# Attention decode: moving P V of one group among the score sums of the next, with K loads one tile ahead at the end

## The chip, the cores and the metric

One core of one Trainium2 chip. Times are device microseconds (us) of one execution. Fast runs are compared with fast runs; the record gives every run of this study as fast. A ratio is the mean time of one kernel's fast runs over that of the kernel before in the same rounds, with a 95% interval, so it is not quite the ratio of the medians quoted beside it. Times inside a profile are counted from the start of its span, the profiled execution. The chain of a page is the work that ended last, followed back step by step to what each piece waited for.

## The reference, cut to what matters

```python
q = (x @ wq).reshape(B, Sq, H, Dh)...          # B=8, Sq=1, H=32, Dh=128
scores = einsum("bhqd,bhkd->bhqk", q, k_cache) * Dh ** -0.5      # k_cache: 8 x 32 x 4096 x 128, bf16
p = softmax(scores)
o = einsum("bhqk,bhkd->bhqd", p, v_cache)                        # v_cache: the same size
a = o.reshape(B, Sq, H * Dh) @ wo
b = gelu(layernorm(x) @ w1 + b1) @ w2 + b2
return g * a + (1 - g) * b                     # g = sigmoid(sum(x * gate_w))
```

K and V are 537 MB together; the four weight matrices (wq, wo, w1, w2) add 20 MB. All of it is read once.

## The kernel before

It works in 64 groups, each of one batch row and 4 heads. A group has a K tile and a V tile of 4 MB (128 partitions, 128 tokens of 128 values each). There are two K buffers and two V buffers. All large loads are issued by SyncE in program order, and each waits until its buffer is free:

```python
def load_k(g):                       # waits for the last product of group g-2
    k_land[g] = op("sync", ... KB[g % 2] <- K, [k_done.get(g - 2)] ...)
def load_v(g):                       # waits for the last P V matmul of group g-2
    t = op("sync", ... VB[g % 2] <- V, [v_done.get(g - 2)] ...)
```

The scores of a group go in four batches. VectorE multiplies K by q (`mult`, 2.28 us), TensorE adds the products up with eight identity matmuls, and VectorE finishes the sum (`reduce`). Then come the softmax, P V and its reduction to one row a head:

```python
def scores(g, between=lambda: None):
    mult(g, 0)
    mult(g, 1)
    for c in range(NCK):             # NCK = 4
        reduce(g, c)
        if c == 0:
            between()                # normalises group g-1
        if c + 2 < NCK:
            mult(g, c + 2)
...
def pv(g):
    ... 32 matmuls P^T V, the first waits for V, the exponentials and the PSUM bank (accumulators) ...
    v_done[g] = p_pv[g]
    ... total (ones x row sums), eviction to O_sb on ScalarE, gather (8 small matmuls) ...
...
for g in range(NG):                  # NG = 64; cut
    ... load_k(g); load_v(g)   (g == 62: load_k(62), load_k(63), load_v(62), V63 in pieces)
    scores(g, between)
    q_of(g + 1)
    softmax(g)                       # 4 exponentials on ScalarE
    ... up projection in groups 2 to 13, down projection in groups 18 to 23 ...
    pv(g)
```

TensorE's order is thus sums of g, P V of g, sums of g+1.

## Time and profile before

| | before |
|---|---|
| median of the first 3 runs (range) | 1367.1 us (1364.4 to 1367.9) |
| span of the profiled run | 1359.6 us |
| busy: TensorE, VectorE, ScalarE | 69%, 61%, 16% |
| mean DMA rate | 410 GB/s |
| last V lands / end | 1340.1 / 1359.6 us |

The prediction below shows the lines of the profile that matter: the chain of waits, the costliest groups, one turn of the loop, and the windows at the end. One line on SyncE, from the waits of the DMA queue of the kernel before (who waited, for whom, total us, times, longest), is of use later:

```profile
SPq L213 <- PE psb L381: 547.6, 59, 10.0
```

SyncE stands in front of a V load (L213) until P V has given the buffer back. The wait alone is no loss, since earlier loads are still running meanwhile. What matters is how far ahead of their end the next load is issued.

### The profile page before, as it was taken

The numbers are of one execution on the slowest core, as the hardware profiler recorded it, in microseconds if no ns is written. First come the engines' busy times: TensorE is split into PE (matmuls) and PEld (weight loads), VectorE is DVE, ScalarE is ACT, GpSimd is POOL, SyncE is SP. The second block draws the span as 40 slices with busy tenths as digits, with TensorE's granted clock in tenths as the row PEclk, the third lists the DMA queues.
The fourth block names the chain that finished last, engine by engine and source line by source line (L and its number), as shares of the span: only waits on it lengthen the run. The fifth ranks groups of instructions, "written<-read, shape, count | busy, mean of one in ns | idle before, by whom it ended". The sixth has DMA issues, their size and how long they took to land.

```text
span 1359.6 us, 12287 instructions
## 1 busy us (share of the span) xinstructions
PE 931.5 (69%) x5166; PEld 420.5 (31%) x5166; DVE 823.9 (61%) x992; ACT 212.0 (16%) x650; POOL 1.8 (0%) x10
## 2 busy tenths in 40 slices
PE   4647777777677777577677676676577676676676
PEld 1223333333233333233233233233233232233232
DVE  3646565565655656665755655755755655655655
ACT  1201111111211111111111111111111111111111
POOL 0000000000000000000000000000000000000000
PEclk9968787887887888987887887987887878877878
DMA  9999999999999999999999999999999999999963
GB/s 387 408 423 432 431 431 431 430 427 403 431 431 431 431 431 397 440 430 430 431 430 429 431 430 421 407 411 402 411 403 410 426 416 405 403 407 416 414 293 155
DMA packets 24598, 557.75 MB, mean 410 GB/s; under 512 B 2368, under 2 KB 6496, under 8 KB 6752
## 3 DMA queue, kind: packets, MB, share of 16 engines
q1 hardware_dynamic: 24368, 556.95, 97.0%
q8 instruction: 40, 0.66, 0.2%
q14 instruction: 14, 0.11, 0.0%
q10 hardware_dynamic: 176, 0.03, 0.0%
HBM read 556.96 MB, written 0.01 MB: 410 GB/s over the span
## 4 chain that ended last, share of the span: by engine, by line
PE 43%; DVE 37%; ACT 13%; DMA 4%; issue 2%; SPq 0%; DVEq 0%
PE psb L340 21%; DVE p L330 21%; PE psb L381 14%; ACT P L370 10%; DVE s_sb L345 9%; PE psb L391 7%; DMA KB<-in_A_k_cache_dram 3%; ACT O_sb L388 3%; DVE mA L361 1%; DMA RB<-in_A_wq_dram 1%; DVE mB L363 1%; DVE mD L367 1%; DVE gm L364 1%; DVE mC L366 1%; PE psb L308 1%
## 5 line engine op out<-in xcount | busy, mean ns | idle before, releaser
L340 PE MATMUL psb<-p,ident 128*128 128x512 bf16 x2048 | 563.8, 432 | 145.9 <-DVE p L330 145.9
L330 DVE TENSOR_TENSOR p<-KB,q_bc 128x4096 bf16<-128x4096 bf16 x256 | 577.4, 2276 | 56.0 <-DMA KB<-in_A_k_cache_dram 34.7
L345 DVE TENSOR_REDUCE s_sb<-psb 128x32 f32<-128x512 f32 x256 | 176.0, 688 | 451.3 <-PE psb L340 451.3
L381 PE MATMUL psb<-VB,P 128*16 128x512 bf16 x2048 | 203.7, 569 | 243.7 <-ACT P L370 243.7
L340 PEld LDWEIGHTS psb<-p,ident 128*128 128x128 bf16 x2048 | 215.7, 113 | 472.9 <-DVE p L330 209.6
L381 PEld LDWEIGHTS psb<-VB,P 128*16 128x16 bf16 x2048 | 65.2, 115 | 345.0 <-issue 332.3
L370 ACT ACTIVATE P<-s_sb,mD 32x128 bf16<-32x128 f32 x256 | 147.1, 575 | 116.1 <-DVE mD L367 113.1
L324 ACT ACTIVATE q_bc<-psb 128x128 bf16<-128x128 f32 x64 | 17.8, 278 | 778.9 <-PE psb L322 778.9
L391 PE MATMUL psb<-sel,O_sb 128*128 128x4 f32 x512 | 95.2, 309 | 19.5 <-ACT O_sb L388 19.5
L391 PEld LDWEIGHTS psb<-sel,O_sb 128*128 128x128 f32 x512 | 89.6, 264 | 25.1 <-ACT O_sb L388 25.1
L388 ACT ACTIVATE O_sb<-psb 128x512 f32<-128x512 f32 x64 | 38.2, 597 | 215.7 <-PE psb L381 215.7
L370 ACT ACTIVATION_READ_ACCUMULATOR P<-s_sb,mD 32x1 f32 x256 | 63.7, 249 | 0.0
L386 PEld LDWEIGHTS psb<-rs,ones 128*128 128x128 f32 x128 | 26.3, 257 | 50.8 <-issue 50.8
L386 PE MATMUL psb<-rs,ones 128*128 128x4 f32 x128 | 32.0, 320 | 0.0
L361 DVE TENSOR_REDUCE mA<-s_sb 128x1 f32<-128x128 f32 x64 | 18.3, 286 | 2.2
L308 PE MATMUL psb<-RB,p 128*8 128x512 bf16 (+1 forms) x40 | 11.6, 418 | 9.1 <-DMA RB<-in_A_wq_dram 9.1
L409 PE MATMUL psb<-yT_sb,RB 128*128 128x8 bf16 (+1 forms) x180 | 17.8, 206 | 0.0
L409 PEld LDWEIGHTS psb<-yT_sb,RB 128*128 128x128 bf16 (+1 forms) x180 | 16.4, 151 | 2.4
L397 DVE RECIPROCAL rz<-psb 128x4 f32<-128x4 f32 x64 | 11.1, 173 | 9.9 <-PE psb L391 9.9
L363 DVE STREAM_TRANSPOSE mB<-mA 128x32 f32<-128x32 f32 x64 | 13.6, 212 | 2.2
L367 DVE STREAM_TRANSPOSE mD<-mC 128x32 f32<-128x32 f32 x64 | 13.6, 212 | 2.2
L322 PE MATMUL psb<-Q,Sel 128*128 128x128 bf16 x64 | 14.0, 219 | 0.0
(56 smaller groups left out, 97.1 us busy)
## 6 DMA issues: line engine op xcount, KB each, us to landing
KB<-in_A_k_cache_dram SPq DMA_DIRECT2D x64, 4096.0 KB, 17.7
VB<-in_A_v_cache_dram SPq DMA_DIRECT2D x63, 4096.0 KB, 18.1
RB<-in_B_w_dram SPq DMA_DIRECT2D x1, 5184.0 KB, 15.3
RB<-in_B_w_dram SPq DMA_DIRECT2D x1, 4608.0 KB, 40.9
RB<-in_A_wo_dram SPq DMA_DIRECT2D x1, 4608.0 KB, 15.4
RB<-in_A_wq_dram SPq DMA_DIRECT2D x1, 4096.0 KB, 12.8
VB<-in_A_v_cache_dram SPq DMA_DIRECT2D x1, 2048.0 KB, 16.9
VB<-in_A_v_cache_dram SPq DMA_DIRECT2D x1, 1024.0 KB, 19.0
```

What stands on the lines that cost most here:

```text
L330: v_mult[g, c] = op("vector", lambda e: e.tensor_tensor(out=p1[:, par, :, :], in0=KB[s][:, c * CT:(c + 1) * CT, :], in1=qb, op=ALU.mult), ...
L340: p_sum[g, c] = op("tensor", lambda e, r=r, n=n: e.matmul(tr_ps[par][:, :], lhsT=ident[:, :], rhs=r, start=(n == 0), stop=(n == NCH - 1)), w)
L345: v_red[g, c] = op("vector", lambda e: e.tensor_reduce(out=s_sb[:, s, c * CT:(c + 1) * CT], in_=tr_ps[par][:, :].rearrange("p (t c) -> p t ...
L361: t = op("vector", lambda e: e.tensor_reduce(out=mA[:, 0:1], in_=s_sb[:, s, :], axis=AX.X, op=ALU.max), [v_red[g, NCK - 1], c_mA])
L363: t = op("vector", lambda e: e.transpose(mB[:, :], mA[:, :]), [t])
L367: v_nm[g] = op("vector", lambda e: e.transpose(mD[:, s, :], mC[:, :]), [t, a_exp.get(g - 2)])
L370: a_exp[g] = op("scalar", lambda e, h=h, q=q: e.activation(out=P[q, s, :, h], in_=s_sb[q, s, :], func=ACT.Exp, bias=mD[q, s, 0:1], scale=1 ...
L381: p_pv[g] = op("tensor", lambda e, o=o, tq=tq: e.matmul(o, lhsT=P[:, s, tq * TQ:(tq + 1) * TQ, :].rearrange("p t h -> p (t h)"), rhs=VB[s] ...
L386: op("tensor", lambda e: e.matmul(oz_ps[:, HB:2 * HB], lhsT=ones[:, :], rhs=rs[:, s, :], start=True, stop=True), [a_exp[g], v_norm.get(g - ...
L388: a_ev[g] = op("scalar", lambda e: e.activation(out=O_sb[:].rearrange("p t d -> p (t d)"), in_=o_ps[s][:, :], func=ACT.Copy), [p_pv[g], p_ ...
L391: p_oz[g] = op("tensor", lambda e, tt=tt: e.matmul(oz_ps[:, 0:HB], lhsT=O_sb[:, tt, :], rhs=sel16[:, tt, :], start=(tt == 0), stop=(tt == ...
L409: st["p_up"] = op("tensor", lambda e, w=w, jt=jt, kt=kt, ksz=ksz: e.matmul(xy_ps[0][:, jt * B:(jt + 1) * B], lhsT=w, rhs=yT_sb[0:ksz, kt, ...
```

## The change

Intent: P V of group g-1 is issued in four quarters, each behind one batch of score sums of group g, so that TensorE never stands in front of P V waiting for exponentials. For the last groups the K loads run one tile ahead of V. The core of the diff (the functions `total`, `evict` and `gather` are cut out of `pv` unchanged):

```diff
+    def scores(g, between):
         mult(g, 0)
+        between(0)
         mult(g, 1)
+        between(1)
         for c in range(NCK):
             reduce(g, c)
-            if c == 0:
-                between()
             if c + 2 < NCK:
                 mult(g, c + 2)
+                between(c + 2)
...
+    K_AHEAD = NG - 2
...
+        if g == K_AHEAD - 1:
             load_k(g)
             load_k(g + 1)
             load_v(g)
-            load_v_pieces(g + 1)
+        elif g == K_AHEAD:
+            load_k(g + 1)
+            load_v(g)
+        elif g > K_AHEAD:
+            load_v_pieces(g)
...
+        def between(c, g=g):
+            if g >= 1 and g < K_AHEAD:
+                pv(g - 1, c, NCK)
+            if c == 1:  ... norm(g - 2), and the two VectorE steps of the MLP ...
+            if c == 2:  ... the share of the up or down projection ...
...
+        if g >= K_AHEAD:
+            softmax(g)
+            pv(g - 1, 0, 1)
+        if g >= 1:
+            total(g - 1)
+            evict(g - 1)
+            gather(g - 1)
+        if g < K_AHEAD:
+            softmax(g)
```

The buffers stay two and two. A V buffer is now held into the next group.

More of the change, by code (lines that the diff above doesn't have):

```diff
@@ L347, in reduce @@
             axis=AX.X, op=ALU.add), [p_sum[g, c], a_exp.get(g - 2)])
-    def scores(g, between=lambda: None):
+    def scores(g, between):
         mult(g, 0)
+        between(0)
         mult(g, 1)
+        between(1)
         for c in range(NCK):
             reduce(g, c)
-            if c == 0:
-                between()
             if c + 2 < NCK:
                 mult(g, c + 2)
+                between(c + 2)
     def softmax(g):
@@ L372, in softmax, with pv @@
                 accum_out=rs[q, s, h:h + 1]), [v_nm[g], p_pv.get(g - 2), c_P, c_rs])
-    def pv(g):
+    def pv(g, part, parts):
         s = g % 2
         for land, t0, t1 in v_land[g]:
+            t0, t1 = max(t0, part * NTT // parts), min(t1, (part + 1) * NTT // parts)
             for tq in range(t0 // TQ, t1 // TQ):
@@ L385, in pv, with total, evict, gather @@
         v_done[g] = p_pv[g]
-        op("tensor", lambda e: e.matmul(oz_ps[:, HB:2 * HB], lhsT=ones[:, :], rhs=rs[:, s, :], start=True, stop=True),
+    def total(g):
+        op("tensor", lambda e: e.matmul(oz_ps[:, HB:2 * HB], lhsT=ones[:, :], rhs=rs[:, g % 2, :], start=True, stop=True),
            [a_exp[g], v_norm.get(g - 1), c_ones])
+    def evict(g):
+        s = g % 2
         a_ev[g] = op("scalar", lambda e: e.activation(out=O_sb[:].rearrange("p t d -> p (t d)"), in_=o_ps[s][:, :],
                                                       func=ACT.Copy), [p_pv[g], p_oz.get(g - 1)])
+    def gather(g):
         for tt in range(TQ):
@@ L465, in bass_gated_mix__mha_block_cached__mixer_channel_mlp__decode_kernel @@
     for g in range(NG):
-        if 2 <= g < NG - 2:
-            load_k(g)
-            load_v(g)
-        elif g == NG - 2:
+        if g == K_AHEAD - 1:
             load_k(g)
@@ L472, in bass_gated_mix__mha_block_cached__mixer_channel_mlp__decode_kernel @@
             load_v(g)
-            load_v_pieces(g + 1)
-        def between(g=g):
-            if g > 0 and (g - 1) in p_oz:
-                norm(g - 1)
-            if g == UP0 + UPN:
-                act_h()
-            if g == DN0 + DNN:
-                b_out()
+        elif g == K_AHEAD:
[3 more added lines that the diff above has]
+            load_v_pieces(g)
+        elif g >= 2:
+            load_k(g)
+            load_v(g)
+        def between(c, g=g):
+            if g >= 1 and g < K_AHEAD:
+                pv(g - 1, c, NCK)
+            if c == 1:
+                if g >= 2 and (g - 2) not in v_norm:
+                    norm(g - 2)
+                if g == UP0 + UPN:
+                    act_h()
+                if g == DN0 + DNN:
+                    b_out()
+            if c == 2:
+                if UP0 <= g < UP0 + UPN:
+                    up_proj((g - UP0) * NJ // UPN, (g - UP0 + 1) * NJ // UPN)
+                if DN0 <= g < DN0 + DNN:
+                    down_proj((g - DN0) * NJ // DNN, (g - DN0 + 1) * NJ // DNN)
         scores(g, between)
@@ L485, in bass_gated_mix__mha_block_cached__mixer_channel_mlp__decode_kernel @@
             q_of(g + 1)
-        softmax(g)
-        if UP0 <= g < UP0 + UPN:
-            up_proj((g - UP0) * NJ // UPN, (g - UP0 + 1) * NJ // UPN)
         if g == UP0 + UPN:
             load_w2()
-        if DN0 <= g < DN0 + DNN:
-            down_proj((g - DN0) * NJ // DNN, (g - DN0 + 1) * NJ // DNN)
         if g == DN0 + DNN:
             load_wo()
-        if g >= AP0 and (done_a + 1) * B <= g:
+        if g >= K_AHEAD:
[7 more added lines that the diff above has]
+            softmax(g)
+        if g >= AP0 and (done_a + 1) * B < g:
             a_proj(done_a)
             done_a += 1
-        if g == NG - 2:
-            continue
-        if g == NG - 1:
-            pv(g - 1)
-            norm(g - 1)
-        pv(g)
+    norm(NG - 2)
+    pv(NG - 1, 0, 1)
+    total(NG - 1)
+    evict(NG - 1)
+    gather(NG - 1)
     norm(NG - 1)
```

## The prediction

> **What bounds the kernel now.** I read four views in this order: the chain of work that ended last, the costliest groups, that chain again for one group near the end, and the DMA over windows. The kernel runs 64 groups; each loads a 4 MB K tile and a 4 MB V tile, forms scores (VectorE products at L330, TensorE sums at L340, VectorE reductions at L345), a softmax (exponentials on ScalarE at L370), and P V on TensorE (L381).
>
> ```profile
> PE 43%; DVE 37%; ACT 13%; DMA 4%; issue 2%; SPq 0%; DVEq 0%
> ...
> L340 PE MATMUL psb<-p,ident 128*128 128x512 bf16 x2048 | 563.8, 432 | 145.9 <-DVE p L330 145.9
> L330 DVE TENSOR_TENSOR p<-KB,q_bc 128x4096 bf16<-128x4096 bf16 x256 | 577.4, 2276 | 56.0 <-DMA KB<-in_A_k_cache_dram 34.7
> ...
> L381 PE MATMUL psb<-VB,P 128*16 128x512 bf16 x2048 | 203.7, 569 | 243.7 <-ACT P L370 243.7
> ```
>
> The reader is to see that DMA is only 4% of the chain although its busy row shows nines nearly throughout, that VectorE waited for K only 34.7 us in all, and that TensorE stood 243.7 us in front of P V, waiting for exponentials. No engine is full (PE 69%, DVE 61%): the loop is a chain that hops from engine to engine. One turn of it:
>
> ```profile
> 1145.51 0.22 DVE mD L367
> ...
> 1147.54 0.58 ACT P L370 x2
> 1148.12 0.14 issue
> 1148.26 3.62 PE psb L381 x29
> 1151.87 0.02 issue
> 1151.90 0.61 ACT O_sb L388
> 1152.50 0.04 issue
> 1152.55 1.87 PE psb L391 x8
> 1154.42 3.45 PE psb L340 x8
> 1157.87 0.02 issue
> 1157.89 0.69 DVE s_sb L345
> ```
>
> Between the end of one softmax and the first reduction of the next group, 12.2 us pass (1145.73 to 1157.89): exponentials 2.4, P V 3.6, eviction 0.6, gather 1.9, and two batches of score sums although VectorE had the products ready at 1150.1. TensorE takes its work in program order, so sums whose operands are there stand behind a P V that waits for ScalarE. That turn took 22.0 us; the one before it, where the TensorE clock was higher, 19.45:
>
> ```profile
> 1126.20:1145.65 19.45, 12.24 (x75) 5.41 (x75) 12.69 (x17) 3.18 (x10) 0.00 (x0) 0.91 0.98 398
> 1145.65:1167.67 22.02, 15.98 (x75) 6.94 (x75) 12.63 (x16) 3.18 (x10) 0.00 (x0) 0.69 0.98 411
> ```
>
> From the product that starts at 615.37 to the one at 1330.47 there are 35 groups: 20.43 us each, and none of them waited for K. How fast could DMA go? Near the start, where a weight load had put K behind, VectorE did wait:
>
> ```profile
> 81.39 4.49 DVE L330 TENSOR_TENSOR p<-KB,q_bc 128x4096 bf16<-128x4096 bf16 x2 [17.29 <-DMA KB<-in_A_k_cache_dram]
> 100.81 4.49 DVE L330 TENSOR_TENSOR p<-KB,q_bc 128x4096 bf16<-128x4096 bf16 x2 [3.54 <-DMA KB<-in_A_k_cache_dram]
> ```
>
> 19.42 us for one K and one V: that is the price of a group when DMA alone sets the pace, and the trace has these loads landing 9.71 or 9.72 us apart in every stretch where the queue stays full. So compute, at 20.43, is only 1.0 us per group above the DMA floor. DMA works off its early backlog at 431 GB/s until some 880 us and then dips to 408. Second place of loss, the end:
>
> ```profile
> 1280.00:1320.00 40.00, 26.60 (x147) 11.75 (x146) 25.14 (x30) 6.37 (x20) 0.00 (x0) 0.83 0.76 313
> 1320.00:1360.00 40.00, 25.55 (x152) 11.50 (x150) 22.39 (x32) 6.08 (x19) 0.00 (x0) 0.84 0.44 188
> ```
>
> K62 has landed at 1300.2; K63 and V62 are issued only at 1307.3, since K63 waits for its buffer and V62 stands behind it. Nothing moves for 8.4 us. The last piece of V lands at 1340.1, and 19.5 us of compute follow.
>
> **What the Trainium skill says.** "DMA: Bandwidth & Descriptors", section "Where 436 GB/s comes from", puts the fabric ceiling at 435 GB/s for 16 engines; the trace's 431 over 160 us agrees. The same section says that for HBM transfers about 358 binds; this trace, with one core running, contradicts that. "TensorE: Matmul & The Clock Gate", section "What's actually happening", says the clock halves after an idle window of about 3.4 us and returns after a busy one. The trace agrees: the 4.46 us wait for exponentials comes once a group, and eight sums then take 3.45 us instead of 1.90. The same page, section "Step-by-step: what each phase is for", says that only weight loads are pulled ahead and matmuls stay in program order, which the waiting sums above show.
>
> **The change part by part.**
> (a) It adds no work and removes none; the same instructions are reordered. P V of group g-1, in four quarters of eight matmuls, follows the four batches of sums of group g. Its exponentials (2.4 us after the softmax) are then done before the first sum (product 2.2 us, sum 1.9 to 3.5) ends. The 4.5 us wait goes, and P V, eviction and gather leave the chain from softmax to next score.
> (b) The new compute turn, from durations above, S being the start of the first product. Full clock: product to 2.2, sum to 4.1, P V quarter (1.9/4) to 4.6, second sum to 6.5; first reduction after the second product (4.5) and a normalisation (0.4), to 5.6; third product to 7.8, second reduction to 8.5, fourth product to 10.7, third reduction to 11.4; fourth sum to 12.6, last quarter to 13.1, last reduction to 13.3, softmax chain 1.15: about 14.5. With the clock at half for the first 10 us (sums 3.5, quarters 0.9): fourth sum ends near 16.5, last quarter 17, turn 18.5. Both are below 19.42, so DMA becomes the bound.
> (c) What the order costs: V buffers come free a group later. V(g+1) may be issued when the last quarter of P V(g-1) is done, at S(g)+13 to +17. In a DMA-bound loop K(g+1) lands at S(g)+19.4, and a load needs about 1.0 us from issue to its first data (1307.3 to 1308.3), so V(g+1) must be issued by S(g)+18.4. Slack 1 to 5 us. In the 12 groups with up projection, 15 matmuls (1.48 us at full clock) now lie among the sums, and in 6 with the down projection 12; there the slack can vanish. I take 3 us in all.
> (d) The DMA floor. The last of the first weight loads lands at 71.96. After it come 124 K or V loads at 9.715: 1204.7. The later weights: 12.4 and 13.0 us, with 2 us of slower neighbours. Hiccups of the kind seen once in some 300 us (one load taking 11.25): 3. The last V in pieces took 10.95 instead of 9.7: 1.2. Sum 1308, against 1340.1.
> (e) The end. With K one tile ahead, K63 needs a buffer free at S(61)+12 and is due in the queue some 7 us later, so the 8.4 us hole closes. Counting back from the landing of V63 at 0, one slot of 9.7 us each: V62 lands at -9.7, K63 at -19.4, V61 at -29.1, K62 at -38.9, K61 at -48.6. Scores of 61 then end at -31.3 (17.4 after K61), those of 62, at full clock, at -17.5, P V(61) at -17.2, which lets V63 be issued 6 us before its turn. Scores of 63 end near -1.6, its exponentials at 0.8, the eviction of 62 at 1.4, the gather at 2.7. From the start of the last P V to the end, before took 9.65 us (1349.95 to 1359.6). Tail: 12.4 us instead of 19.5.
> Sum: 1308 + 12.4 + 3 = 1323.4 for the profiled span, against 1359.6. The timed runs of before lie some 3 to 6 us over its profiled time of 1361.4; I add 4 and say 1327, 2.9% less.
>
> **The rivals.**
> V buffers become the bound: two periods hold one V wait, so the period is (time to the last quarter + 1.0 + 19.4)/2. It passes 19.42 only if the last quarter ends later than 18.4 after S. For it: TensorE at half clock for whole groups would make sums and quarters alone 17.6 us, ending at 19.8. Against: in before each cold stretch was 3.4 or 10.2 us. If it held everywhere: 20.1 a group, some 40 us more, so about the time of before.
> Nothing gained in the loop since DMA is already at 97%: then only the end improves, 8.4 + 7 us, giving 1352. For it: the row of nines. Against: 20.43 against 19.42 with no wait on K.
> DMA faster than I think: 440 GB/s windows of a few us are seen, but none over 40 us goes past 432. If it did, compute would set the pace, and with 18.5 us a turn (1.9 less in some 50 groups) the time would be about 1270; I hold that for very unlikely.
>
> **Range and chances.** The floor of 1308 plus the shortest tail and no losses gives about 1316 timed. Losses of 0.3 us a group would give 1346. The line for 2% is at 1339.8, 13 us above my figure. Hence 1316 to 1345, and 0.80, 0.18, 0.02.
>
> **What would show it.** Right: the chain is mostly DMA on K; VectorE's wait for K grows from 34.7 us to some 200 or more; the 243.7 us wait of P V on exponentials is nearly gone; DMA holds 428 to 431 to the last 20 us; K63 lands without a hole; groups start 19.4 us apart. Wrong: VectorE or P V waiting on late V or K with GB/s near 410 (the V rival), SyncE waiting on P V just before holes, or groups of 20 us with no DMA wait.

## The result, and the profile after

The changed kernel took 1333.0 us (median of 4; 1330.7 to 1335.1) against 1365.8 for the kernel before in the same rounds: ratio 0.9764, interval 0.9733 to 0.9796. In a later job, on the same yardstick, it came to 0.9787 (0.9770 to 0.9803). So it is 2.1 to 2.4% faster, 2.0 to 2.7% with the intervals; by the 2% line of the record the first measurement is "faster" and the second "unclear".

From the page of the changed kernel, the chain by engine and line, and the costliest groups (in the changed kernel P V is L384):

```profile
DMA 60%; PE 21%; DVE 18%; ACT 1%; issue 1%; SPq 0%; DVEq 0%
...
L340 PE MATMUL psb<-p,ident 128*128 128x512 bf16 x2048 | 600.4, 446 | 380.7 <-DVE p L330 378.0
L330 DVE TENSOR_TENSOR p<-KB,q_bc 128x4096 bf16<-128x4096 bf16 x256 | 579.5, 2284 | 281.6 <-DMA KB<-in_A_k_cache_dram 258.9
...
L384 PE MATMUL psb<-VB,P 128*16 128x512 bf16 x2048 | 171.0, 418 | 0.0
```

Three readings. The chain went from 4% DMA to 60%. P V waits for nothing (0.0 instead of 243.7 us), and ScalarE fell from 13% of the chain to 1%. VectorE now waits 258.9 us for K, in 60 places, instead of 34.7. The compute loop now has slack: it stops in front of each K until it lands. One turn by the timeline of the changed kernel (start, duration, engine, line, operation; in brackets the idle time before it), TensorE, K's first product and the loads:

```profile
1016.37 4.49 DVE L330 TENSOR_TENSOR p<-KB,q_bc 128x4096 bf16<-128x4096 bf16 x2 [4.16 <-DMA KB<-in_A_k_cache_dram]
1018.72 3.60 PE L340 MATMUL psb<-p,ident 128*128 128x512 bf16 x8 [5.88 <-DVE p L330]
...
1022.24 0.73 PE L384 MATMUL psb<-VB,P 128*16 128x512 bf16 x8
...
1022.91 1.90 PE L340 MATMUL psb<-p,ident 128*128 128x512 bf16 x8
...
1024.74 0.61 PE L384 MATMUL psb<-VB,P 128*16 128x512 bf16 x8
...
1029.92 0.61 PE L384 MATMUL psb<-VB,P 128*16 128x512 bf16 x8
...
1030.58 0.33 SPq L213 DMA_DIRECT2D VB<-in_A_v_cache_dram  x1
...
1030.95 0.43 SPq L207 DMA_DIRECT2D KB<-in_A_k_cache_dram  x1
```

The last quarter ends at 1030.5, 14.2 us after the first product; right then SyncE issues the next V, and the next K directly behind it, which was ready earlier but stands behind V in the queue. The turn (first product to the end of the softmax on VectorE) takes 15.2 to 16.3 us in most groups without a projection (17.0 in group 14, 17.3 in the last), and up to 17.7 with one. All are below the 19.42 us that two loads take.

SyncE's own waits in the changed kernel tell the new dependence. The profile puts this wait down to L322, the matmul next to the last quarter on TensorE:

```profile
SPq L213 <- PE psb L322: 1146.3, 60, 35.8
```

V loads now wait 1146.3 us for TensorE instead of 547.6. The number alone is no loss: K loads, which now stand behind V, waited 657.6 us for VectorE before and wait 44.8 now. It says that P V decides when both loads are issued. Part of the gain is lost where that is too late, as the experiments show. The rate over the up-projection groups (120 to 320 us) and over a stretch without projections, from windows of the changed kernel (busy us of the engines, then clock, DMA share and GB/s):

```profile
120.00:320.00 200.00, 146.45 (x900) 62.85 (x900) 128.66 (x150) 30.14 (x99) 0.00 (x0) 0.80 0.99 417
...
600.00:1240.00 640.00, 431.89 (x2492) 163.91 (x2496) 419.49 (x491) 101.03 (x330) 0.00 (x0) 0.79 1.00 429
```

417 against 429 GB/s: the early stretch is not at the DMA's rate, although its share reads 0.99. And the end:

```profile
1300.00:1320.00 20.00, 14.43 (x110) 6.37 (x108) 14.54 (x21) 3.88 (x13) 0.00 (x0) 0.91 0.85 358
1320.00:1340.00 20.00, 7.37 (x58) 4.17 (x58) 1.65 (x6) 2.80 (x8) 0.00 (x0) 0.77 0.00 0
```

The last V lands at 1319.5 (before: 1340.1), and 13.8 us of compute follow (before: 19.5). Of the 26.3 us that the span lost, 20.6 are an earlier end of the DMA and 5.7 a shorter end.

### The profile page after: what moved, and what is told of

Read it like the earlier page. It is cut to its first block, busy times and chain, and to the rows that moved or that the text cites. A ratio compares the mean times of both kernels' runs of the same rounds, so it can differ in the third digit from the quotient of the medians.

```text
span 1333.3 us, 12286 instructions
## 1 busy us (share of the span) xinstructions
PE 885.7 (66%) x5166; PEld 346.8 (26%) x5166; DVE 833.0 (62%) x992; ACT 205.1 (15%) x650; POOL 1.8 (0%) x10
## 2 busy tenths in 40 slices
DMA packets 24598, 557.75 MB, mean 418 GB/s; under 512 B 2368, under 2 KB 6496, under 8 KB 6752
## 4 chain that ended last, share of the span: by engine, by line
DMA 60%; PE 21%; DVE 18%; ACT 1%; issue 1%; SPq 0%; DVEq 0%
DMA KB<-in_A_k_cache_dram 59%; PE psb L340 16%; DVE p L330 13%; DVE s_sb L345 4%; PE psb L384 2%; DMA RB<-in_A_wq_dram 1%; PE psb L308 1%; PE psb L419 1%; DVE mA L363 0%; ACT P L372 0%; PE psb L444 0%; PE psb L401 0%; ACT O_sb L396 0%; PE psb L465 0%; DVE mB L365 0%
## 5 line engine op out<-in xcount | busy, mean ns | idle before, releaser
L340 PE MATMUL psb<-p,ident 128*128 128x512 bf16 x2048 | 600.4, 446 | 380.7 <-DVE p L330 378.0
L330 DVE TENSOR_TENSOR p<-KB,q_bc 128x4096 bf16<-128x4096 bf16 x256 | 579.5, 2284 | 281.6 <-DMA KB<-in_A_k_cache_dram 258.9
L340 PEld LDWEIGHTS psb<-p,ident 128*128 128x128 bf16 x2048 | 203.7, 110 | 735.1 <-DVE p L330 430.8
L324 ACT ACTIVATE q_bc<-psb 128x128 bf16<-128x128 f32 x64 | 17.7, 277 | 1036.5 <-PE psb L322 1036.5
L384 PE MATMUL psb<-VB,P 128*16 128x512 bf16 x2048 | 171.0, 418 | 0.0
L401 PE MATMUL psb<-sel,O_sb 128*128 128x4 f32 x512 | 68.0, 256 | 47.7 <-ACT O_sb L396 47.7
L401 PEld LDWEIGHTS psb<-sel,O_sb 128*128 128x128 f32 x512 | 62.4, 192 | 53.3 <-ACT O_sb L396 53.3
L384 PEld LDWEIGHTS psb<-VB,P 128*16 128x16 bf16 x2048 | 28.9, 86 | 128.5 <-issue 127.1
L391 PE MATMUL psb<-rs,ones 128*128 128x4 f32 x128 | 21.7, 240 | 0.0
L391 PEld LDWEIGHTS psb<-rs,ones 128*128 128x128 f32 x128 | 20.0, 196 | 1.3 <-issue 1.3
L419 PE MATMUL psb<-yT_sb,RB 128*128 128x8 bf16 (+1 forms) x180 | 18.4, 209 | 0.0
L322 PE MATMUL psb<-Q,Sel 128*128 128x128 bf16 x64 | 14.7, 229 | 0.0
## 6 DMA issues: line engine op xcount, KB each, us to landing
VB<-in_A_v_cache_dram SPq DMA_DIRECT2D x1, 2048.0 KB, 12.5
```

The lines of the kernel that those rows point to most:

```text
L324: a_qb[g] = op("scalar", lambda e: e.activation(out=q_bc[:, g % 2, :], in_=qb_ps[:, 0:DH], func=ACT.Copy), [t, v_mult.get((g - 2, NCK - 1))])
L330: v_mult[g, c] = op("vector", lambda e: e.tensor_tensor(out=p1[:, par, :, :], in0=KB[s][:, c * CT:(c + 1) * CT, :], in1=qb, op=ALU.mult), ...
L340: p_sum[g, c] = op("tensor", lambda e, r=r, n=n: e.matmul(tr_ps[par][:, :], lhsT=ident[:, :], rhs=r, start=(n == 0), stop=(n == NCH - 1)), w)
L384: p_pv[g] = op("tensor", lambda e, o=o, tq=tq: e.matmul(o, lhsT=P[:, s, tq * TQ:(tq + 1) * TQ, :].rearrange("p t h -> p (t h)"), rhs=VB[s] ...
L391: op("tensor", lambda e: e.matmul(oz_ps[:, HB:2 * HB], lhsT=ones[:, :], rhs=rs[:, g % 2, :], start=True, stop=True), [a_exp[g], v_norm.get ...
L401: p_oz[g] = op("tensor", lambda e, tt=tt: e.matmul(oz_ps[:, 0:HB], lhsT=O_sb[:, tt, :], rhs=sel16[:, tt, :], start=(tt == 0), stop=(tt == ...
```

## The experiments

My theory had three parts. (1) Deferring P V past its exponentials takes the compute chain under the DMA floor, and this is nearly the whole gain. (2) What is missing to the floor is lost because V is issued too short a time before the loads ahead of it run out. (3) The time after the last load is a compute chain that starts with K61. Rivals: the gain is the DMA hole at the end; before was DMA-bound anyway; the missing time is noise of the memory; quarters matter as such.

I use two quantities, both from the issue and landing times in the traces. The *lead* of V(g) is the landing of the load before it, K(g), minus the issue of V(g). The *excess* is the spacing of two landings less 9.715 us, the spacing in a full queue; it is summed over K2 to V62.

### One part of the change alone

e1 keeps P V in quarters to the last group and loads K and V in plain turn:

```diff
-    K_AHEAD = NG - 2
+    K_AHEAD = NG
-        if g == K_AHEAD - 1: ...            # K one tile ahead
+        if 2 <= g < NG - 1:   load_k(g); load_v(g)
+        elif g == NG - 1:     load_k(g); load_v_pieces(g)
```

> P V in quarters for all groups, K and V loaded in plain turn to the end. My theory (P V taken out of the chain lets the loop fall to the DMA floor; the K order only shortens the end): the loop as in the changed kernel, groups 19.4 to 20 us apart, K63 one slot later, so some 4 to 7 us more than the changed kernel, about 1338. Rival (most of the gain is the end, where 8.4 us of DMA stood still): about 1355.

Measured: 1337.4 us, ratio 0.9803 (0.9789 to 0.9816). Most groups are 19.4 to 20 us apart (up to 21.3 in the projection groups, and some 32 at two weight loads), the last V lands at 1316.7, and the time after it is 18.9 us instead of 13.8. So the moved P V alone makes nearly the whole difference. The K order shortens the end by 5 us in the trace. In the timed ratios it is worth 2 to 5 us, depending on which of the two measurements of the changed kernel is taken; against the second, the intervals overlap.

e2 is the kernel before with only the K order at the end:

```diff
-        elif g == NG - 2:
-            load_k(g); load_k(g + 1); load_v(g); load_v_pieces(g + 1)
+        elif g == NG - 3:
+            load_k(g); load_k(g + 1); load_v(g)
+        elif g == NG - 2:
+            load_k(g + 1); load_v(g)
+        elif g == NG - 1:
+            load_v_pieces(g)
```

> The kernel before with only the load order of the end changed (K one tile ahead). My theory: the compute chain of 20.4 us a group set the pace to the end, the hole of 8.4 us in the DMA lay beside it, so within 2 us of before, 0.998 to 1.002. Rival (the hole was lost time): 8 us less or more, 0.994 or below.

Measured: ratio 0.9997 (0.9985 to 1.0009), median 1363.3. So this order alone is worth nothing. But e2 does not test a closed hole: its trace shows the hole one group earlier. Now K62 waits for its buffer with V61 behind it, and no data moves from 1282.7 to 1289.6:

```profile
1283.00:1289.00 6.00, 4.79 (x17) 1.62 (x16) 5.97 (x7) 0.00 (x0) 0.00 (x0) 0.84 0.00 0
```

That the hole of 8.4 us, which I had called a place of loss, cost nothing is read from the trace of the kernel before: K63 lands at 1319.5, and its first product begins only at 1330.5, behind the softmax of group 62; the last V lands at 1340.1, and its P V begins only at 1350.0.

### Was before bound by compute, and is after bound by DMA?

e6 and e7 halve the V bytes from the third group on, in the kernel before and in the changed one. The results are wrong on purpose: half of each V buffer keeps old data. (The comparison with the reference passed all the same. Attention averages 4096 small values here, so passing says little about P V; no run here tests it more finely.)

```diff
-        t = op("sync", ... VB[s][:, :, :] <- src ...)
+        n = NTT if g < 2 else NTT // 2
+        t = op("sync", ... VB[s][:, 0:n, :] <- src[:, 0:n, :] ...)
-    V_LAST = (64, 32, 16, 16)
+    V_LAST = (64,)
```

> Wrong result on purpose: the kernel before, V loads of 2 MB instead of 4 from the third group on (the other half of the buffer keeps old data). Theory (compute chain of 20.4 us a group sets the pace of before): only the early waits on K and the time after the last V shrink, 1335 to 1362, a ratio over 0.975. Rival (before was bound by DMA, as its busy row suggests): a quarter of the bytes gone, 1060 to 1150.

> Wrong result on purpose: the changed kernel with the same halved V loads. Theory (the changed loop is bound by DMA, its compute turn is 15.2 to 17.7 us by the trace): groups 15.5 to 16.5 us apart, 1090 to 1140 in all. Rival (the changed loop is bound by its own waits, such as P V on V or the clock): above 1250.

Measured: e6 1363.4 us, ratio 1.0001 (0.9988 to 1.0015). Taking away 130 of 558 MB changes nothing. e7 1144.0 us, ratio 0.8386 (0.8370 to 0.8402). The same cut takes some 190 us off the changed kernel; its groups are then 15.0 to 17.4 us apart but for the two weight loads (15.5 to 16.5 were expected). The upper end of my range (1140) was missed by 4 us. The chain by engine, first of e6, then of e7:

```profile
PE 44%; DVE 36%; ACT 13%; DMA 4%; issue 2%; SPq 0%; DVEq 0%
```

```profile
DMA 46%; PE 29%; DVE 23%; issue 1%; ACT 1%; SPq 0%; DVEq 0%
```

e6 has the chain of the kernel before to a per cent, though its DMA moved only 427 MB in the same time. This is the test that the nines in the DMA row could not give: DMA was busy in the kernel before because there was just enough to do, not because the end waited for it.

### What is missing to the floor

Two kernels give V back earlier in the projection groups only, or its first half earlier in all groups. e3 moves the projections behind the gather:

```diff
-            if c == 2: ... up_proj(...) / down_proj(...)        # inside between()
...
             gather(g - 1)
+        if UP0 <= g < UP0 + UPN:  up_proj(...)
+        if DN0 <= g < DN0 + DNN:  down_proj(...)
```

> The changed kernel with the two projections after the gather instead of among the sums. Theory (V is issued too late in just the 18 groups with a projection; some 8 to 10 us of excess between landings there): V4 to V14 and V20 to V24 land 9.7 us apart, time 5 to 9 us below the changed kernel, about 1325. Rival (the excess is noise of the memory, not of late issues): no change beyond 2 us.

Measured: 1325.7 us, ratio 0.9713 (0.9696 to 0.9731), against 0.9764 of the changed kernel: 7 us less, as expected (10 us against its second measurement, 0.9787). The excess of K and V in the 18 projection groups falls from 11.1 to 4.2 us, that of V alone from 8.9 to 0.9. It does not vanish everywhere: V17, issued with a lead of 5.2 us, still lands 1.7 us late.

e4 loads each V as two halves with semaphores of their own; the first waits only for the first two quarters of the P V that frees it:

```diff
+        ta = op("sync", ... VB[s][:, 0:hf, :] ..., [v_half.get(g - 2)], ...)
+        tb = op("sync", ... VB[s][:, hf:NTT, :] ..., [v_done.get(g - 2)], ...)
+        v_land[g] = [(ta, 0, hf), (tb, hf, NTT)]
```

> The changed kernel with every V loaded as two halves, the first of which waits only for the first two quarters of P V(g-2's successor in that buffer), so some 7 us sooner. Theory (late V issue): the holes close though the projections stay where they are, 5 to 10 us below the changed kernel. Rival (smaller transfers cost as much as they save, or the excess is not from late issues): equal or slower.

Measured: 1328.9 us, ratio 0.9739 (0.9724 to 0.9754): faster than the changed kernel by 3 to 7 us, a little less than hoped; against the first of its two measurements the intervals overlap. The windows of e4, at the same places as above:

```profile
120.00:320.00 200.00, 144.50 (x901) 62.61 (x902) 131.10 (x152) 33.36 (x107) 0.00 (x0) 0.82 1.01 429
```

429 instead of 417 GB/s with the projections where they were, so it was the issue of V and not the projection's work as such. That e4 stays behind e3 is not clear of noise (the intervals overlap). Its V packets are half as long and there are more packets in all (33670 instead of 24598). In the trace the median packet of 16 KB takes 613 ns, so two take 1226, where one of 32 KB takes 1213; and though its leads are near 10 us, V lands a median 0.07 us late each time (e5 below: 0.00), some 4 us over 60 loads. No run tests packet size alone.

e5, e10 and e11 do P V whole, behind the second, third or fourth batch of sums. Nothing else differs among them, and the projections stay among the sums:

```diff
             if g >= 1 and g < K_AHEAD:
-                pv(g - 1, c, NCK)
+                if c == 1:                  # e5; e10: c == 2; e11: c == 3
+                    pv(g - 1, 0, 1)
```

> The changed kernel with P V of the last group not in quarters but whole, after the second batch of sums; projections stay among the sums. Theory (what counts is that P V is deferred past its exponentials, and that V is given back early enough; quarters as such buy nothing): V is issued near 9.5 us after the first product instead of 14 to 16, the holes of the projection groups close, 5 to 10 us below the changed kernel, about 1324. If the small excesses seen elsewhere also came from an issue only 5 us ahead, nearer 1318. Rival (quarters are needed so that the sums are not held up): slower than the changed kernel, above 1335.

> The changed kernel once more, as the yardstick of the next two on the same chip: ratio 0.974 to 0.979.

> P V whole after the third batch of sums, ahead of the projections: V is given back near S + 12, so a lead of about 7 us over the landing of the K before it. If the excess depends on the lead (none at 9 us, some at 5, much under 4), excess of K and V together 6 to 9 us and time 1 to 3 us over that with P V after the second batch, ratio 0.971 to 0.974. Rival (the order or grouping of P V among the sums matters, not the lead): no such grading.

> P V whole after the fourth batch, behind the projections: given back near S + 15 to 17, later than in quarters, since all four parts come at the end. If the lead decides: excess at least that of the changed kernel (19 us), more in the 18 projection groups, ratio 0.977 to 0.984. Rival (P V whole is better than quarters in itself): below the changed kernel.

Measured (leads are medians; "end" is the time from the last landing to the end of the span; excess, landing and end are of the profiled run):

| kernel | lead, projection / other groups | excess | last V lands | end | median, ratio |
|---|---|---|---|---|---|
| e11, whole, fourth batch | 3.9 / 4.2 us | 28.2 | 1329.3 | 12.5 | 1350.5, 0.9922 |
| changed kernel | 4.2 / 5.2 | 17.8 | 1319.5 | 13.8 | 1333.0, 0.9764 |
| changed kernel again | 4.2 / 5.2 | 14.0 | 1316.4 | 14.3 | 1334.1, 0.9787 |
| e3, projections moved | 5.2 / 5.2 | 9.8 | 1311.0 | 14.4 | 1325.7, 0.9713 |
| e10, whole, third batch | 6.7 / 6.7 | 4.2 | 1308.9 | 16.1 | 1325.0, 0.9722 |
| e5, whole, second batch | 9.4 / 9.4 | 4.3 | 1306.7 | 15.7 | 1324.2, 0.9713 |

The windows of e5, at the same places as those of the changed kernel:

```profile
120.00:320.00 200.00, 139.50 (x904) 69.83 (x905) 132.65 (x152) 32.57 (x105) 0.00 (x0) 0.81 1.00 430
...
600.00:1240.00 640.00, 416.64 (x2525) 185.02 (x2522) 421.69 (x492) 101.24 (x330) 0.00 (x0) 0.77 1.00 430
```

430 GB/s in both stretches. The three kernels differ in one position in TensorE's order, and the time follows the lead. Quarters as such buy nothing: whole P V is faster than quarters when it stands early (e5, e10) and slower when it stands late (e11), which fells the rival that grouping matters. Memory noise is out too, since the excess goes away with a larger lead. Over the V loads of the eight traces with moved P V and full V tiles in one transfer (V3 to V60, without V15 and V25, which stand beside a weight load; the eight are the six of the table, e1 and e8; worked out from their issue and landing times):

```
lead of V      loads   mean excess of V   loads over 0.15 us late
under 4 us        37       0.68 us              76%
4 to 5           106       0.22                 33%
5 to 6           124       0.07                 10%
6 to 7            65       0.00                  0%
8 and more       115       0.03                  2%
```

My expectation for e10 (excess 6 to 9 us) was too cautious: there is no grading above a lead of 6 us. The time of e11 was under-expected (0.977 to 0.984 forecast, 0.9922 measured). Its profiled run took 1343.6 us and fits its excess; its other five runs took 1350 to 1360, and no profile shows where those lost more.

### The end

e8 is e5 with K one tile ahead from one group earlier, and in the last three groups P V and eviction of the group before ahead of the softmax:

```diff
-    K_AHEAD = NG - 2
+    K_AHEAD = NG - 3
...
-        if g >= K_AHEAD:
-            softmax(g)
-            pv(g - 1, 0, 1)
+        if g >= K_AHEAD:
+            pv(g - 1, 0, 1)
         ... total(g - 1), evict(g - 1), gather(g - 1) ...
-        if g < K_AHEAD:
-            softmax(g)
+        softmax(g)
```

> e5 with K one tile ahead from one group earlier, and at the end P V and eviction of the last group but one ahead of the last softmax. Theory (after the last loads the tail of 13.8 us is a compute chain that begins with K61, so an earlier K61 shortens it): tail 6 to 9 us, 5 to 8 us below e5. Rival (the tail hangs on the last V alone): same as e5 within 2 us.

Measured: 1317.8 us, ratio 0.9666 (0.9652 to 0.9680); 6.4 us below e5. The last V lands at 1307.1 as in e5, and the end takes 8.9 instead of 15.7 us. The windows of e8 at the end:

```profile
1300.00:1320.00 20.00, 10.57 (x99) 5.32 (x96) 3.42 (x12) 3.51 (x10) 0.00 (x0) 0.78 0.21 87
```

VectorE has only 3.42 us of work left there, where the changed kernel, whose last V lands 12.4 us later, had 14.54. The last reduction of scores ends at 1302.0, 5.1 us before the last V; in the changed kernel it ended at 1318.0, 1.5 us before. e8 changes the K order and the place of the softmax together; no run separates them. e8 is the fastest kernel of the study, 1.0 to 1.2% below the changed one.

## Why the prediction was right, and where it was off

The forecast was 1327 us in a range of 1316 to 1345, faster by over 2% with 0.80; measured 1333.0 and 0.9764. Step by step:

- *What bounds before* (compute, 20.43 us a group against 19.42 of DMA): right. e6 shows it most plainly, with 1.0001.
- *"Second place of loss, the end"*: wrong as a statement on the kernel before. The hole of 8.4 us lay beside the compute chain: K63 waited 11.0 us for its first product after it. It would probably have become a loss only once the loop was DMA-bound; no run shows that.
- *The turn before*: one slip. The 12.2 us from softmax to first reduction hold one batch of sums, not two: the line at 1154.42 has eight matmuls, and 2.4 + 3.6 + 0.6 + 1.9 + 3.45 with the gaps is the 12.2.
- *(a) and (b), the new turn*: right. 15.2 to 17.7 us were measured for the 14.5 to 18.5 forecast, the wait on exponentials is gone, and e7 shows that groups can follow each other at 15.0 to 17.4.
- *(c), what the order costs*: the mechanism was right and the size was not; this is the term that was mis-sized. I took 1.0 us from issue to first data as all the lead that a load needs, gave V until S + 18.4, and put down 3 us. In the traces the queue loses time at leads under 6 us, that is, beyond some S + 13.4 (19.42 less 6). The issue came at S + 13.8 to 16.3. The loss is the excess of the changed kernel over that of e5: 17.8 - 4.3 = 13.5 us in the first profile, 9.7 in the second. Landing at full rate takes more than first data: the shortest 4 MB load of the kernel before took 12.2 us from issue to landing, against 9.7 in a full queue, so 2.5 us go with starting and ending it. Another part can be seen in the traces: a load reports its landing in 16 semaphore increments, and in K3 to K60 of the changed kernel the first comes a median 2.7 us (at most 3.6) before the last. If the DMA engine that is done first runs dry, 2.5 and 2.7 to 3.6 add up to 5.2 to 6.1, near the lead of 6. That sum is an estimate from these numbers; no run tests it.
- *(d), the DMA floor of 1308*: right to 1.3 us. e5, whose queue is never short, lands its last V at 1306.7. The changed kernel lands it at 1319.5.
- *(e), the end*: 12.4 forecast, 13.8 measured; the counted-back chain held. (V63 was to be issued "6 us before its turn"; the forecast's own -17.2 and -9.7 make 7.5, and 7.6 were measured.)
- *The sum*: 1308 + 12.4 + 3 gave 1323.4 for the span; measured 1333.3, of which 11.5 is the landing and 1.4 the end, less the 3 that I had put down. The 4 us that I added for timed runs over the profiled one were not there: the timed median lies 2 us below the profiled run. That error hid part of the one in (c): the span was missed by 9.9 us and the timed run by only 6, so part of the closeness is luck.
- *The rivals*: the V-buffer rival was thought to need the half clock for whole groups. It was partly true without that, and one sign named for it, SyncE waiting on P V just before holes, came in the projection groups (417 GB/s). The rival "only the end improves" falls with e1, and "DMA faster" with the 430 GB/s of e5.

Still open: why e11's timed runs exceed its profiled one. Untested: K issued ahead of V, or V from another engine's queue, so that K, which is ready earlier, need not stand behind it.

## What to carry to other kernels

A DMA row full of nines doesn't prove a DMA bound: halve the bytes of one operand and see whether the time moves. When a reordering takes an engine's wait away by holding a buffer longer, work out the lead at which the freed buffer's load is issued, and compare it with a lead at which loads really join without a gap in the trace, not with the time to first data. And place the work that frees a buffer as early as its inputs allow: here whole P V after the second batch of sums beat quarters spread over all four.

## What the Trainium skill lacked or had wrong

- "DMA: Bandwidth & Descriptors", section "Where 436 GB/s comes from", says that about 358 GB/s binds for HBM transfers, and that sentence names no condition. With one core running, 430 GB/s were held over 640 us (e5), so it does not hold as it stands; the same paragraph's own 425 GB/s and its 435 for the fabric fit.
- "DMA: Bandwidth & Descriptors", section "Latency and other measured facts", gives about 600 ns to the first byte. No page says how long before the end of the running loads the next one has to be issued if none of the 16 engines is to run dry. Here 4 MB loads from one queue joined without loss at a lead of 6 us or more (but for the late ones of the next point), lost 0.2 us on average at 4 to 5 us, and 0.7 us under 4 us. From issue to first data the kernel before took 1.0 us (1307.3 to 1308.3), 0.6 of it after the issuing instruction had ended (1307.6), so this trace agrees with the 600 ns.
- No page that I read mentions it: in e5 and in e8 the same three loads land 1.3 to 1.6 us late though their queue was full (K13 near 297 us, K38 near 810, V51 near 1074). In each, one of the 16 increments falls 1.3 to 1.6 us further behind the others. In e5 an instruction fetch (queue q8, 16 KB) starts within the 10 us before each of these landings (288.7, 807.8 and 1071.5), but 37 other fetches go by without a late landing. The cause is unknown.
